# Moving the wait for the output's arrival from SyncE to the engine that owns the section

**Chip, cores, metric.** One core of a Trainium2 chip. The metric is the device time of one execution, in microseconds (us). Some words are used throughout. "Landing" is the moment when the last store's semaphore has its full count. A "section" is a stretch of the program in which each engine has its own list of instructions, and its "owner" is the engine that lets the others leave. An engine leaves with an "exit drain", an instruction that raises its "mark", a semaphore that the owner waits for. The "end barrier" is GpSimd's instruction, after the section, that waits for a count of all engines.

## The reference

Two decode steps of attention with one query token and 32 heads of 128. A reads all 16384 keys and values of its cache, B the last 4096 of its own. The two results, 512 numbers each, stand side by side.

```python
q = (x @ wq).reshape(B, Sq, Hq, Dh).transpose(0, 2, 1, 3)
scores = einsum("bhqd,bhkd->bhqk", q, k) * (Dh ** -0.5)
o = einsum("bhqk,bhkd->bhqd", softmax(scores), v)
y = o.transpose(0, 2, 1, 3).reshape(B, Sq, Hq * Dh) @ wo     # A: all keys; B: k, v cut to the last 4096
return concatenate([a, b], axis=-1)
```

## The kernel before

The kernel writes out each engine's instructions in one critical section with semaphores of its own, and names GpSimd as the section's owner. SyncE issues all large loads and, at the end, the two stores of 1 KB. GpSimd makes masks, then only passes semaphores on from VectorE to TensorE.

```python
ctx.enter_context(tc.tile_critical(sync_engine=mybir.EngineType.Pool))   # GpSimd (Pool) owns the section
...
def _sync_program(nc, cx, loads):
    e = nc.sync
    ...                                     # all loads of caches and weights
    for st in cx.sts:
        st.s_row.wait(e, len(st.out_at))
        cx.s_end.on(e.dma_start(out=cx.out[0, 0:1, st.at : st.at + st.DN],
                                in_=cx.row[0:1, st.at : st.at + st.DN]), 16)
    cx.s_end.wait(e, 32)                    # the wait that the change moves
...
def _pool_program(nc, cx):
    e = nc.gpsimd
    ...                                     # masks, zeros
    for i in range(stA.L + stB.L):
        m = _parts(i)
        for _ in range(m):
            n += 1
            cx.s_half.wait(e, n)            # wait and increment: one record of 17 ns
            e.sem_inc(cx.s_add.h, NB // m)
```

The softmax here doesn't subtract the row's maximum and nothing guards it: scores larger than these inputs give would overflow.

## Time and profile before

| | before |
|---|---|
| device time, median of 3 runs | 822.25 us (822.18 to 822.5) |
| span of the profiled run | 820.0 us |
| share of the 16 DMA engines' time filled by SyncE's queue | 99.4% |
| bytes moved | 352.41 MB at 430 GB/s |
| from the landing of the last store to the end of the span | 1.13 us |

What an engine does on leaving the section can be read in the view of one source line: engine, operation, count, then shortest, median and longest record in ns, and first and last start in us. The boundary's drains, no-ops and semaphore instructions are put down to L512.

```profile
L512 POOLq EVENT_SEMAPHORE  x3: 17/43/43, 778.3 to 819.1; - x3
L512 POOLq NOP  x2: 13/13/13, 0.8 to 819.2; - x2
L512 POOLq DRAIN  x1: 41/41/41, 778.4 to 778.4; - x1
L512 PEldq DRAIN  x1: 430/430/430, 816.9 to 816.9; - x1
L512 ACTq DRAIN  x1: 396/396/396, 817.3 to 817.3; - x1
L512 DVEq DRAIN  x1: 459/459/459, 817.3 to 817.3; - x1
L512 SPq DRAIN  x1: 13/13/13, 819.1 to 819.1; - x1
```

GpSimd (POOLq) runs its first boundary instruction and its own exit drain at 778.3 and 778.4 us, 40 us before the end. TensorE, ScalarE and VectorE drain at 817, while the output is still under way. Only SyncE's drain, at 819.1, stands behind the landing.

### The profile page before, as it was taken

The numbers are of one execution on the slowest core, as the hardware profiler recorded it, in microseconds if no ns is written. First come the engines' busy times: TensorE is split into PE (matmuls) and PEld (weight loads), VectorE is DVE, ScalarE is ACT, GpSimd is POOL, SyncE is SP. The second block draws the span as 40 slices with busy tenths as digits, with TensorE's granted clock in tenths as the row PEclk, the third lists the DMA queues.
The fourth block names the chain that finished last, engine by engine and source line by source line (L and its number), as shares of the span: only waits on it lengthen the run. The fifth ranks groups of instructions, "written<-read, shape, count | busy, mean of one in ns | idle before, by whom it ended". The sixth has DMA issues, their size and how long they took to land. (4 is left out here: it accounts for less than half of the span.)

```text
span 820.0 us, 5953 instructions
## 1 busy us (share of the span) xinstructions
PE 341.2 (42%) x2149; PEld 128.6 (16%) x2149; DVE 603.8 (74%) x167; ACT 35.5 (4%) x134; POOL 4.3 (1%) x14
## 2 busy tenths in 40 slices
PE   3433346152424244352608071534243353616276
PEld 1110112020101011110202020211011121202022
DVE  2089995959595968768595959595959969696921
ACT  0100000000000000000000000000000001010110
POOL 2000000000000000000000000000000000000000
PEclk9855668595856675656766575958566766756589
DMA  9999999999999999999999999999999999999997
GB/s 384 436 457 412 457 412 457 412 454 416 454 416 451 416 451 419 451 419 448 422 441 429 435 435 428 441 419 451 416 454 411 456 412 435 435 435 435 435 423 325
DMA packets 8222, 352.41 MB, mean 430 GB/s; under 512 B 916, under 2 KB 920, under 8 KB 1304
## 3 DMA queue, kind: packets, MB, share of 16 engines
q1 hardware_dynamic: 8212, 352.33, 99.4%
q8 instruction: 4, 0.07, 0.0%
q14 instruction: 2, 0.02, 0.0%
q10 hardware_dynamic: 4, 0.00, 0.0%
HBM read 352.32 MB, written 0.00 MB: 430 GB/s over the span
## 5 line engine op out<-in xcount | busy, mean ns | idle before, releaser
L304 DVE TENSOR_TENSOR kt<-kt,qallA 128x32768 bf16<-128x32768 bf16 (+2 forms) x20 | 276.2, 13810 | 150.7 <-DMA kt<-in_A_k_cache_dram 150.7
L379 PE MATMUL acc<-vt,p 128*8 128x512 bf16 (+1 forms) x1216 | 113.1, 550 | 348.3 <-PEq L42 348.3
L379 PE MATMUL red<-kt,ident 128*128 x640 | 183.2, 457 | 43.1 <-PEq L42 43.1
L315 DVE TENSOR_TENSOR kt<-kt 128x16384 bf16<-128x16384 bf16 (+2 forms) x24 | 174.5, 7269 | 0.8
L379 PEld LDWEIGHTS acc<-vt,p 128*8 128x8 bf16 (+1 forms) x1216 | 37.1, 114 | 423.5 <-issue 416.5
L379 PEld LDWEIGHTS red<-kt,ident 128*128 128x128 bf16 x640 | 72.5, 113 | 150.3 <-issue 103.6
L304 DVE TENSOR_TENSOR kt<-kt,qallB 128x16384 bf16<-128x16384 bf16 x8 | 69.5, 8691 | 13.4 <-DMA kt<-in_B_k_cache_dram 13.4
L321 DVE TENSOR_REDUCE sc<-red 128x256 f32<-128x2048 f32 x20 | 45.7, 2284 | 8.0 <-PE red L379 8.0
L233 ACT ACTIVATE p<-sc,offA 128x256 bf16<-128x256 f32 x32 | 16.0, 500 | 604.5 <-DVE sc L321 604.5
L379 PE MATMUL f<-s,win 128*32 128x128 f32 x48 | 11.2, 323 | 62.4 <-PEq L42 62.4
L379 PE MATMUL red<-vt,kt 128*128 128x512 bf16 x64 | 16.1, 416 | 4.6 <-DMA vt<-in_A_wq_dram 2.5
L233 ACT ACTIVATE p<-sc,offB 128x128 bf16<-128x128 f32 x32 | 12.4, 389 | 113.4 <-DVE sc L321 113.4
L342 DVE TENSOR_REDUCE s<-acc 128x128 f32<-128x512 f32 x24 | 16.6, 691 | 0.8
L379 PEld LDWEIGHTS f<-s,win 128*32 128x32 f32 x48 | 4.2, 121 | 72.9 <-issue 72.6
L337 DVE TENSOR_TENSOR acc<-acc,maskA 128x512 f32<-128x512 f32 x16 | 11.1, 692 | 0.0
L335 DVE COPY win<-selB 128x32 f32<-128x32 f32 x8 | 1.4, 178 | 11.3 <-PE acc L379 11.3
L379 PEld LDWEIGHTS red<-vt,kt 128*128 128x128 bf16 x64 | 6.6, 105 | 13.7 <-issue 7.8
L379 PE MATMUL red<-vt,ocA 128*1 128x512 bf16 x32 | 7.2, 379 | 0.0
L379 PE MATMUL acc<-kt,p 128*16 128x512 bf16 x64 | 5.3, 505 | 4.3 <-PEq L42 4.3
L335 DVE COPY win<-selA 128x32 f32<-128x32 f32 x16 | 2.8, 174 | 5.4 <-PE acc L379 5.4
L233 ACT ACTIVATION_READ_ACCUMULATOR p<-sc,offB 128x1 f32 x32 | 6.0, 187 | 0.0
L233 ACT ACTIVATION_READ_ACCUMULATOR p<-sc,offA 128x1 f32 x32 | 6.0, 187 | 0.0
(47 smaller groups left out, 36.8 us busy)
## 6 DMA issues: line engine op xcount, KB each, us to landing
kt<-in_B_k_cache_dram SPq DMA_DIRECT2D x8, 4096.0 KB, 34.8
vt<-in_B_v_cache_dram SPq DMA_DIRECT2D x6, 4096.0 KB, 29.0
kt<-in_B_v_cache_dram SPq DMA_DIRECT2D x2, 4096.0 KB, 36.6
vt<-in_A_wq_dram SPq DMA_DIRECT2D x1, 4096.0 KB, 12.2
vt<-in_B_wq_dram SPq DMA_DIRECT2D x1, 4096.0 KB, 21.4
vt<-in_A_wo_dram SPq DMA_DIRECT2D x2, 2048.0 KB, 23.1
vt<-in_B_wo_dram SPq DMA_DIRECT2D x1, 2048.0 KB, 29.7
vt<-in_B_wo_dram SPq DMA_DIRECT2D x1, 1024.0 KB, 31.6
```

The costliest lines, as they stand in the source:

```text
L233: ins = e.activation(out=p[:, :, g, :], in_=cx.sc[:, u * st.keys : (u + 1) * st.keys].rearrange("p (t e) -> p t e", e=4), func=ACT.Exp, sc ...
L304: n = did(e.tensor_tensor(out=k, in0=k, in1=q.rearrange("p (o d) -> p o d", o=1).broadcast_to([P, b - a, DH]), op=ALU.mult,))
L315: cx.s_half.on(e.tensor_tensor(out=k[:, :, 0 : DH // 2], in0=k[:, :, 0 : DH // 2], in1=k[:, :, DH // 2 : DH], op=ALU.add,))
L321: cx.s_sc.on(e.tensor_reduce(out=cx.sc[:, :], in_=cx.red[:, :, :].rearrange("p b (k w) -> p (b k) w", w=W), axis=AX.X, op=ALU.add,))
L335: did(e.tensor_copy(cx.win[u][:, :], st.sel[:, at : at + H]))
L337: n = did(e.tensor_tensor(out=acc, in0=acc, in1=st.mask[:, :].rearrange("p (x o) -> p x o", o=1).broadcast_to([P, 4, DH]), op=ALU.mult,))
L342: cx.s_pick.on(e.tensor_reduce(out=cx.s[u][:, :], in_=acc.rearrange("p x d -> p d x"), axis=AX.X, op=ALU.add,))
L379: mm = lambda *a, **k: e.matmul(*a, skip_group_check=True, **k)
```

## The change

Its intent: GpSimd closes the section, so let it wait for the output itself. SyncE then need not wait and tell GpSimd.

```diff
 def _sync_program(nc, cx, loads):
     ...
         cx.s_end.on(e.dma_start(...), 16)
-    cx.s_end.wait(e, 32)

 def _pool_program(nc, cx):
     ...
             e.sem_inc(cx.s_add.h, NB // m)
+    cx.s_end.wait(e, 32)
```

## The prediction

> **What bounds the kernel now.** I read the page first, for the engine that limits, then the chain of waits that ended last, then the waits of SyncE's queue, then stretches of the tail, and last the records of single instructions there.
>
> ```profile
> span 820.0 us, 5953 instructions
> PE 341.2 (42%) x2149; PEld 128.6 (16%) x2149; DVE 603.8 (74%) x167; ACT 35.5 (4%) x134; POOL 4.3 (1%) x14
> DMA  9999999999999999999999999999999999999997
> DMA packets 8222, 352.41 MB, mean 430 GB/s; under 512 B 916, under 2 KB 920, under 8 KB 1304
> ...
> q1 hardware_dynamic: 8212, 352.33, 99.4%
> ```
>
> All sixteen DMA engines are busy in every slice but the last, and SyncE's queue fills 99.4% of their time at 430 GB/s. The two caches and the weights are 352 MB: 352.41 MB / 430 GB/s = 819.6 us, which is the span. POOL (GpSimd) computes for 4.3 us of 820 and then only passes semaphores on. So the body is bound by bytes, and the change touches none of them. What it can move is the time after the last weight has landed:
>
> ```profile
> by line: DMA vt<-in_B_wo_dram 4.0%; PE acc L379 0.4%; SPq L171 0.3%; DVE row L373 0.1%; PE red L379 0.0%; issue 0.0%
> ...
> 784.12 32.74 DMA vt<-in_B_wo_dram
> 816.86 0.04 issue
> 816.90 0.40 PE red L379 x4
> 817.30 0.03 issue
> 817.33 0.42 DVE row L373
> ```
>
> The chain of what ended last stops at 817.75 us, where the last half row of B is in SBUF. Between that and 820.0 lie 2.25 us, in which the result is stored and the program closed.
>
> ```profile
> SPq L174 <- DVE row L373: 6.0, 1, 6.0
> SPq L132 <- DMA out_dram<-row: 0.9, 1, 0.9
> SPq L566 <- PEq L566: 0.5, 2, 0.4
> ...
> 817.00:818.00 1.00, 0.28 (x4) 0.00 (x0) 0.42 (x1) 0.37 (x1) 0.00 (x0) 1.00 0.00 0
> 818.00:819.00 1.00, 0.00 (x0) 0.00 (x0) 0.00 (x0) 0.00 (x0) 0.00 (x0) 1.00 0.00 1
> 819.00:820.00 1.00, 0.00 (x0) 0.00 (x0) 0.00 (x0) 0.00 (x0) 0.00 (x0) 0.74 0.00 0
> ```
>
> The first three lines are SyncE's queue: after its last issue (L174) it waits 0.9 us for the output's arrival, and this wait is attached to a branch printed as L132. In the last 2 us no compute engine does anything. The wait the change moves is 0.9 us out of 820, or 0.1%.
>
> [...] SyncE's branch has a record of only 33 ns although it had waited 0.9 us, so I count from start to start. [...] here the store took 818.874 - 817.772 = 1.10 us from issue to landing, so the measurement is used, and who waits cannot shorten it. [...] Here SyncE needs 160 ns from its branch to its next instruction, against 74 ns between its two later semaphore instructions, so a branch costs 86 ns more[...].
>
> **The change part by part.** The records of the semaphore instructions at the end, from the trace (start in us, length in ns; the meaning of each semaphore is my reading of who raises it and who waits):
>
> ```text
> GpSimd 778.248  17  last pass to TensorE
> GpSimd 778.326  17  raises "owner is through" (four engines' exit drains wait for it)
> GpSimd 778.422  41  its own exit drain, raises its mark
> SyncE  817.772 249  issues the store of B
>        818.874      both stores have landed
> SyncE  818.891  33  branch out of the section, held till then
> SyncE  819.051  13  exit drain, raises its mark (seen 819.065)
> GpSimd 819.089  43  second of two waits for the engines' marks (first: 817.831)
> GpSimd 819.176  13  no-op
> GpSimd 819.219  34  drain
> SyncE  819.353   7  drain, raises the end barrier's count (819.361)
> GpSimd 819.385  17  end barrier, has all the counts
>        820.004      last engine past the second end barrier
> ```
>
> The section's owner matters: GpSimd raises "owner is through" at the end of its own list, 40 us before the end, and the drains by which SyncE, ScalarE, VectorE and TensorE leave wait for it. Moving the wait into GpSimd's list puts it in front of that signal.
>
> Removed: SyncE's 0.9 us wait. Its branch and its 160 ns now follow the issue, from about 818.02 to 818.2, beside the store. SyncE's hop to GpSimd goes too: 819.089 - 819.051 = 38 ns.
>
> Added on GpSimd: a wait for 32 on the store's semaphore. I expect it to merge into the instruction that raises "owner is through", as each of the 24 earlier waits of that loop merged into one 17 ns record with its increment. It starts at 818.874 + 17 (SyncE's reaction) = 818.891.
>
> Moved behind the landing, GpSimd's line of instructions: the exit drain 96 ns later (778.326 to 778.422), 818.987. The first wait for marks about 85 ns later (the 34 ns drain at 819.743 is followed 78 ns later, this drain is 7 ns longer), 819.072. The second wait 87 ns later (as 819.089 to 819.176), 819.159. No-op 87, 819.246; drain 43, 819.289. The end barrier 78 ns after that, 819.367. Before it was 819.385. So the estimate is 18 ns earlier.
>
> Do the other engines' marks arrive in time? "Owner is through" goes out at 818.891; the end barrier's release, also raised by GpSimd, went from 819.464 to the waiters at 819.505 to 819.517, so 41 to 53 ns. The four drains start at 818.93 to 818.95, take about 10 ns as in the end barrier and are seen by 819.0: before GpSimd's waits at 819.07 and 819.16. Does SyncE then hold the barrier? From its drain at 818.93 to its count are 310 ns in the trace (819.051 to 819.361): 819.24, before 819.367. So GpSimd's line alone sets the end.
>
> Sum, both from 818.891. Old: 160 (branch) + 38 (hop) + 87 + 43 + 166 (from GpSimd's drain to the end barrier, 78 of it the usual gap and 88 spent waiting for SyncE's count) = 494 ns. New: 96 + 85 + 87 + 87 + 43 + 78 = 476 ns. Common to both are 87 + 43 + 78; what is saved is 160 + 38 + 88 = 286 ns, what is added is 96 + 85 + 87 = 268 ns. Change -0.02 us, with an error of some 0.1 us from the gaps I borrowed.
>
> **The rivals.**
> First, the handoff really is saved: if the exit marks and GpSimd's drain cost less than borrowed, or the author's idea holds that the owner has only its last no-op left, the gain is at most 819.176 - 818.891 = 0.285 us, 0.03%. The record of "owner is through" speaks against it.
> Second, the release costs more than it saves: the wait becomes an instruction of its own (+80 ns, the spacing of GpSimd's semaphore instructions), or an idle engine's exit drain is slow. TensorE took 430 ns, ScalarE 396, VectorE 459 in those drains, but each was then finishing real work; if they took that when idle, GpSimd would get its marks at 818.95 + 0.46 = 819.41 rather than 819.07, and the end moves by 0.25 us later, 822.5.
> Third, the change reaches the loads: if it shifted the instruction streams so that an issue came late, every percent of DMA idleness would be 8 us. The issues of the loads are the same instructions before the changed line, and the loads' waits are untouched; I give this almost nothing.
> Fourth, the end is hidden anyway: the measured 822.25 us is 2.25 us over the span[...].
>
> **Range and chances.** 822.25 - 0.02 rounds to 822.2 us. The rivals span 822.25 - 0.29 = 821.96 to about 822.5. The runs of before alone spread from 822.18 to 822.5, 0.32 us, so the state of a run is worth more than the effect. With 0.3 us added on each side the range is 821.7 to 822.8. A verdict of faster or slower needs 16 us, over fifty times what any rival makes: 0.005 each, 0.99 within 2%.
>
> **What would show it.** Right: the tail's records show GpSimd held until the store lands, the four exit drains starting together 40 to 50 ns later, SyncE's branch near 818.0 (on this trace's clock), its waits list without the 0.9 us on the output's arrival, and the end barrier within 0.1 us of 511 ns after landing (before: 819.385 - 818.874); DMA still at 99.4%. Wrong: exit drains that start before the landing (then the owner's signal isn't behind the wait), drains of hundreds of ns on idle engines, or a time outside 821.7 to 822.8 with the tail unchanged, which would put the cause in the loads or in the run itself.

Its sum: 494 ns for the old tail and 476 for the new, so -0.02 us and a forecast of 822.2 us.

## The result, and the profile after

| | before | after |
|---|---|---|
| device time, median of 6 runs | 822.26 us (822.0 to 822.5) | 822.3 us (822.2 to 822.48) |
| ratio | | 1.0001, 95% interval 0.9988 to 1.0014 |
| landing to end barrier, first profile | 511 ns | 688 ns |
| the same, second profile | 511 ns | 688 ns |

A ratio is the mean time of one kernel's fast runs over that of the other's of the same rounds, so not quite the ratio of the medians. The time is the same. The tail, the stretch from the landing to the end barrier, became 0.18 us longer, which is less than the spread of the runs.

First the page of the changed kernel:

```profile
span 820.5 us, 5953 instructions
PE 341.7 (42%) x2149; PEld 128.8 (16%) x2149; DVE 603.8 (74%) x167; ACT 35.5 (4%) x134; POOL 4.3 (1%) x14
DMA  9999999999999999999999999999999999999997
DMA packets 8222, 352.41 MB, mean 430 GB/s; under 512 B 916, under 2 KB 920, under 8 KB 1304
...
q1 hardware_dynamic: 8212, 352.33, 99.3%
```

As many instructions, as many packets, the same busy times to a few tenths of a microsecond: the body didn't change. The span is 0.45 us longer in this profile, but its last result (the end of "row") already came 0.27 us later, at 818.02 against 817.75, ahead of anything that was changed. A second profile of the kernel before has a span of 820.7 us. Spans of the body wander by such amounts, and the tail has to be measured from the landing.

The waits of SyncE's queue after the change:

```profile
SPq L174 <- DVE row L373: 5.4, 1, 5.4
SPq L512 <- POOLq L512: 1.1, 1, 1.1
...
SPq L566 <- PEq L566: 0.7, 2, 0.4
```

The 0.9 us on the output's DMA are gone, and in their place SyncE waits 1.1 us for GpSimd at the section's boundary. The wait was not removed but turned: SyncE now waits for the engine that waits for the store. The store itself took 1.10 us from issue to landing in the first profile of either kernel. The branch that carries the wait, and the boundary's line, both of the changed kernel:

```profile
L132 POOLq COMPARE_BRANCH  x1: 33/33/33, 819.2 to 819.2; - x1
```

```profile
L512 POOLq EVENT_SEMAPHORE  x3: 17/43/43, 819.3 to 819.6; - x3
L512 POOLq NOP  x2: 13/13/13, 0.8 to 819.7; - x2
L512 SPq DRAIN  x1: 13/13/13, 819.4 to 819.4; - x1
L512 ACTq DRAIN  x1: 8/8/8, 819.4 to 819.4; - x1
L512 DVEq DRAIN  x1: 17/17/17, 819.4 to 819.4; - x1
L512 PEldq DRAIN  x1: 8/8/8, 819.4 to 819.4; - x1
L512 POOLq DRAIN  x1: 41/41/41, 819.4 to 819.4; - x1
```

Compare the starts with those of before. Everything that stood at 778 or 817 us now stands at 819.3 or later: GpSimd's first signal, its drain, and the drains of all four other engines, which that signal releases (they start 42 to 53 ns after it). The drains of TensorE, ScalarE and VectorE have become short, 8 to 17 ns instead of 396 to 459. In the kernel before, those of ScalarE and VectorE ended 35 and 52 ns after the engine's last operation; now the last operation is over 1.3 us before them. They cost little: the other engines' marks are all raised by 252 ns after the landing, and GpSimd's first wait for them starts only at 389. GpSimd's own row of instructions is what costs, 516 ns from its signal to the end barrier.

The single records, counted in ns from the landing, show the sum:

```text
before: SyncE waits                       after: GpSimd waits
   17  SyncE   branch                       24  GpSimd  branch
  177  SyncE   exit drain                  172  GpSimd  raises "owner is through"
  215  GpSimd  second wait for marks       214  SyncE   exit drain (others: 218 to 225)
  302  GpSimd  no-op                       268  GpSimd  exit drain
  345  GpSimd  drain                       389  GpSimd  first wait for marks
  511  GpSimd  end barrier                 480  GpSimd  second wait for marks
                                           567  GpSimd  no-op
                                           610  GpSimd  drain
                                           688  GpSimd  end barrier
```

### The profile page after: what moved, and what is told of

It reads as the page before. It is cut to its first block, busy times and chain, and to the rows that moved or that the text cites. A ratio compares the mean times of both kernels' runs of the same rounds, so it can differ in the third digit from the quotient of the medians.

```text
span 820.5 us, 5953 instructions
## 1 busy us (share of the span) xinstructions
PE 341.7 (42%) x2149; PEld 128.8 (16%) x2149; DVE 603.8 (74%) x167; ACT 35.5 (4%) x134; POOL 4.3 (1%) x14
## 2 busy tenths in 40 slices
DMA packets 8222, 352.41 MB, mean 430 GB/s; under 512 B 916, under 2 KB 920, under 8 KB 1304
## 3 DMA queue, kind: packets, MB, share of 16 engines
q1 hardware_dynamic: 8212, 352.33, 99.3%
## 5 line engine op out<-in xcount | busy, mean ns | idle before, releaser
L379 PE MATMUL acc<-vt,p 128*8 128x512 bf16 (+1 forms) x1216 | 111.3, 543 | 350.0 <-PEq L42 350.0
L379 PE MATMUL red<-vt,kt 128*128 128x512 bf16 x64 | 18.2, 455 | 4.6 <-DMA vt<-in_A_wq_dram 2.5
```

The lines of the kernel that those rows point to most:

```text
L379: mm = lambda *a, **k: e.matmul(*a, skip_group_check=True, **k)
```

## The experiments

The theory: behind the landing stands a row of sequencer instructions with fixed distances, and the owner that waits puts its whole row there. Rivals: the two tails differ by chance; GpSimd alone is slow; the tail is hidden by the closing of the program. For edits of a single line the diff is against the kernel named.

### before_again and after_again: is the tail's length chance?

No edit, one look each.

> The kernel before once more, for the repeatability of its tail. Theory 1 (the tail is fixed instruction spacing): from the landing of the last store to GpSimd's end barrier 511 ns as in the first profile, within 20 ns, whatever the span does. Theory 2 (the tail is as noisy as the span, and the 511 against 688 ns of the two first profiles is chance): it differs from 511 by 50 ns or more.

> The changed kernel once more. Theory 1: 688 ns from landing to end barrier, within 20 ns. Theory 2: it differs from 688 by 50 ns or more, perhaps down to 511.

Measured: 511 and 688 ns, as in the first profiles, to the nanosecond, while the times were 822.8 and 822.4 us, the wrong way round. So single runs can't rank these kernels, and the tail can.

### owner_plain and sync_plain: what does the branch cost?

```diff
# owner_plain, against the changed kernel; sync_plain: the same in SyncE's list, against the kernel before
     cx.s_end.wait(e, 32)
+    e.sem_inc(cx.s_own.h, 1)    # nobody waits for it
```

> GpSimd waits, but an increment of a semaphore that nobody waits on follows the wait, so that the wait sits on a plain semaphore instruction and not on the branch out of the section. Theory 1 (the branch is what the prediction mis-sized, 148 ns from its start to the next instruction against 78 for a plain one): landing to end barrier 688 - 70 = 618 ns, no branch record on GpSimd. Rival (GpSimd is slow to leave a wait of any kind): stays within 20 ns of 688, or gets longer by the added instruction's 78 ns.

> The kernel before with the same added increment after SyncE's wait. Theory 1: SyncE's 160 ns from its branch to its exit drain become about 75 to 95 ns, landing to end barrier 511 - 75 = 436 ns, within 25 ns: the shortest tail so far. Rival: 511 or more, since the added instruction costs what the branch did.

Measured: 618 and 416 ns, with times of 822.25 and 822.51 us. In owner_plain the wait sits on a 17 ns semaphore record and the next instruction follows after 78 ns instead of 148; the rest keeps its distances. In sync_plain SyncE's drain follows after 74 ns instead of 160. So in these kernels an instruction added makes the tail shorter: the wait that was last in its list sat on the branch out of the section, and the branch cost 70 ns more than the increment on GpSimd (148 - 78) and 86 on SyncE (160 - 74). But the owner's tail without the branch (618) is still above the old one with it (511), so the branch is only part of the 177 ns: with the branch gone on both sides, 618 against 416, the owner's tail is still 202 ns longer.

### owner_tail26 and owner_ahead26: does the tail reach the measured time?

```diff
# owner_tail26, against the changed kernel; in owner_ahead26 the loop stands ahead of the wait
     cx.s_end.wait(e, 32)
+    for _ in range(26):
+        e.sem_inc(cx.s_own.h, 1)
```

> GpSimd waits, then does 26 increments that nobody waits on. Theory 1 (GpSimd's instructions behind the landing reach the measured time one for one): landing to end barrier 688 - 148 + 26 x 78 = 2.57 us, the time 1.9 us over the changed kernel, 824.2 us. Rival (the end of the program is hidden behind the launch's own closing): the time stays within 0.5 us of 822.3.

> The same 26 increments ahead of GpSimd's wait, where it is idle for 40 us. Both theories: landing to end barrier 688 ns within 20, time 822.3 within 0.4 us. If it were longer, the number of instructions and not their place would count.

Measured over 4 runs each: owner_tail26 824.23 us (824.14 to 824.32), ratio to before 1.0024, interval 1.0008 to 1.0039; owner_ahead26 822.22 us (821.87 to 822.51), ratio 1.0001. The tails are 2949 and 693 ns. The same 26 instructions cost 2.0 us behind the landing and nothing ahead of it, so the tail isn't hidden. One line of SyncE's waits in owner_tail26 says it:

```profile
SPq L514 <- POOLq L514: 3.3, 1, 3.3
```

SyncE waits 3.3 us for the owner's signal, where it waited 1.1 in the changed kernel. The tail of 2949 ns missed the expected 2570: the increments follow one another by 78 ns, but after the same one of them, the twenty-first, the next comes 441 ns later in both kernels. The traces show where it stands. Counted from the start of the trace, this is the step after GpSimd's 68th record, behind the landing in one kernel and 39 us ahead of it in the other. The two kernels with twelve sections, below, have a long step after the 68th record as well (440 ns where GpSimd waits, 424 where SyncE waits), and the first of them has another, of 403 ns, after the 196th, 128 records on. The other kernels have at most 61 records of GpSimd and no such step. So in these four kernels the place went by the count of GpSimd's records, 68, and not by where the landing lay; that such a step comes again after 128 records was seen once. What fills the gap was not shown: both kernels with 26 increments moved one packet more on queue 14, which the page marks "instruction", than the kernel before (3 instead of 2, 8192 bytes each), but it began 0.69 us after the gap's end in owner_tail26 and 4.25 us after it in owner_ahead26. The time grew by 2.0 us where the tail grew by 2.26; the difference of 0.25 us is within the spread of the four runs.

### twelve_sync and twelve_owner: thirteen exits instead of one

```diff
# after the main section, in both; the last line's engine is nc.sync or nc.gpsimd,
# and the main section is that of the kernel before or of the changed one
+    section.close()
+    for r in range(1, 13):
+        with tc.tile_critical(sync_engine=mybir.EngineType.Pool):
+            for e in (nc.vector, nc.scalar, nc.tensor, nc.gpsimd):
+                e.sem_inc(cx.s_own.h, 1)
+            cx.s_end.on(nc.sync.dma_start(out=..., in_=cx.row[...]), 16)     # B's half again
+            cx.s_end.wait(nc.sync, 32 + 16 * r)
```

> Twelve more sections at the end, each storing B's half of the output again, with an increment on every other engine so that all five take part; SyncE waits for each store, as before. The result stays right. Theory 1: each section costs issue and landing (1.1 us), exit and entry, about 2 us, so some 24 us more than before, near 846 us. The number wanted is the difference from the next run.

> The same twelve sections, with GpSimd waiting for each store. Theory 1 (0.18 us per exit, the whole of it on the path and in the time): 13 x 0.177 = 2.3 us longer than twelve_sync. Rival A (what the exit loses, the next entry gives back, or it lies beside something outside the span): within 0.5 us of twelve_sync. Rival B (the author's intent, a saved hop): shorter than twelve_sync.

Measured over 5 runs each: 842.94 us (842.82 to 843.38; ratio to before 1.0253, interval 1.0239 to 1.0267) and 846.64 us (846.53 to 847.25; ratio 1.0296, interval 1.0282 to 1.031). The owner's wait is slower by 3.70 us. The direction is that of the theory and the effect now stands clear of the spread; Rivals A and B fall. The size was expected at 2.3 us. In the traces the distance from a landing to the next section's store is 622 ns with SyncE waiting and 892 with GpSimd (median of 12), so 270 ns for exit and entry rather than 177 for exit and end barrier: 12 x 0.27 = 3.2 us. The last exit adds 0.6 us (1069 against 466 ns from landing to end barrier), for in twelve_owner the gap of 403 ns lies ahead of its no-op, where the exits before it have 87 to 92. Together that is 3.8 us in the profiled runs, of which 0.3 are this gap; it stands after GpSimd's 196th record, and that it has to do with the wait is not shown. Also here the waits of SyncE's queue, first twelve_sync, then twelve_owner:

```profile
SPq L544 <- DMA out_dram<-row: 10.4, 12, 1.0
```

```profile
SPq L544 <- POOLq L544: 12.8, 12, 1.1
...
SPq L574 <- POOLq L544: 3.7, 12, 0.3
```

Twelve waits for the store, 10.4 us together, became twelve for GpSimd, 12.8 us, and twelve further ones of 0.3 us for GpSimd's mark at the next entry, which the list of twelve_sync doesn't have.

### sync_owner and act_waits: the role or the engine?

```diff
# sync_owner, against the kernel before
-    ctx.enter_context(tc.tile_critical(sync_engine=mybir.EngineType.Pool))
+    ctx.enter_context(tc.tile_critical(sync_engine=mybir.EngineType.SP))
# act_waits, against the kernel before: the wait taken out of SyncE's list, to the end of ScalarE's
+    cx.s_end.wait(e, 32)
```

> SyncE owns the section and waits itself: owner and waiter are one engine, as in the changed kernel, but the engine is SyncE. Theory 1 (what counts is that the owner's release of the four exit drains, and its own exit line, stand behind the wait): the same order of records as in the changed kernel, drains of the other engines after the landing, landing to end barrier about 570 ns (17 + 150 + 90 + 3 x 74 + 60 + 8 + 24), more than the 511 of before and less than 688, since SyncE's instructions follow one another faster. Rival (GpSimd alone is the trouble, an owner that waits is no worse): 511 or less.

> GpSimd owns the section, ScalarE waits for the stores in SyncE's place. Theory 1 (a waiter that doesn't own the section leaves the owner's release and exit drain early): landing to end barrier 511 within 60 ns, GpSimd's owner signal near 778 us as in before. Rival (SyncE alone can wait cheaply): nearer to 688.

Measured: 655 and 388 ns, times of 822.31 and 822.41 us. In sync_owner the records have the order of the changed kernel: SyncE's branch at 17 ns, its signal at 180, the others' drains at 218 to 225, its own row up to 630, the end barrier at 655. GpSimd's drain, at 778 us in the kernel before, stands behind the landing (819.0) here too:

```profile
L512 SPq EVENT_SEMAPHORE  x3: 17/28/28, 819.2 to 819.4; - x3
L512 POOLq DRAIN  x1: 41/41/41, 819.2 to 819.2; - x1
```

That another engine as waiting owner is also slower than 511 says that the role matters, not GpSimd's speed alone. The expected 570 ns, which counted on SyncE's steps of 74 ns where GpSimd's took 78 (both in the kernel before), was too low. act_waits fell outside its expected 511 within 60 ns, on the short side. There SyncE's own closing row, which GpSimd's end barrier waited for until 479 ns in the kernel before, runs beside the store nearly to its end: only two drains are left, and its last count goes out at 316 ns. So the changed kernel's idea, to free SyncE of the wait, does shorten the tail, but in these runs it took a waiter that isn't the owner.

### act_plain: the two helpful edits together

```diff
# against act_waits
     cx.s_end.wait(e, 32)
+    e.sem_inc(cx.s_own.h, 1)
```

> The two helpful edits together: ScalarE waits (it owns nothing, and SyncE's own closing list then lies beside the store), and an increment follows the wait, so that it doesn't sit on the branch. Theory 1: 388 ns from landing to end barrier less the branch's 156 - 78 = 78 ns, so 310 ns within 25: the shortest tail of all, 0.2 us below the kernel before and 0.38 below the changed one. In the measured time 0.2 us are less than the spread of the runs (0.4 us), so the verdict is same, 822.1 us within 0.4. Rival: GpSimd or SyncE becomes the last, 360 ns or more.

Measured: 320 ns, the shortest tail of all. ScalarE's branch had taken 156 ns to the next instruction, the increment in its place took 88: the 68 ns between 388 and 320. In time 822.17 us (821.91 to 822.26, 5 runs), ratio to before 0.9998, interval 0.9984 to 1.0012: the same. No version beats the kernel before by anything that its time shows. Its boundary line:

```profile
L513 POOLq EVENT_SEMAPHORE  x3: 17/43/712, 778.5 to 818.5; - x3
L513 POOLq NOP  x2: 13/13/13, 0.8 to 819.3; - x2
L513 POOLq DRAIN  x1: 41/41/41, 778.6 to 778.6; - x1
...
L513 SPq DRAIN  x1: 218/218/218, 818.3 to 818.3; - x1
L513 ACTq DRAIN  x1: 8/8/8, 819.2 to 819.2; - x1
```

GpSimd's signal and drain are back at 778 us, SyncE's drain is at 818.3, before the landing at 819.1, and of the exit drains only ScalarE's, of 8 ns, stands behind it. The record of 712 ns is GpSimd's second wait for marks, SyncE's and ScalarE's; in act_waits this record, there of 778 ns, runs from 24 ns after SyncE's mark to 30 ns after ScalarE's. So this wait for two semaphores lies inside its record, while SyncE's branch in the kernel before waited 0.9 us and has a record of 33 ns. A record's start, from which the prediction counts, is here not the moment of the last mark.

The tails side by side:

| run | waits | owns | wait sits on | landing to end barrier |
|---|---|---|---|---|
| after, after_again | GpSimd | GpSimd | branch | 688 ns |
| sync_owner | SyncE | SyncE | branch | 655 ns |
| owner_plain | GpSimd | GpSimd | increment | 618 ns |
| before, before_again | SyncE | GpSimd | branch | 511 ns |
| sync_plain | SyncE | GpSimd | increment | 416 ns |
| act_waits | ScalarE | GpSimd | branch | 388 ns |
| act_plain | ScalarE | GpSimd | increment | 320 ns |

## Why the prediction was right, and which step of it was not

- **The bound**: right. The body is bound by bytes: DMA share 99.3 against 99.4%, the same packets, the same time within 0.04 us of medians. 822.3 us lies in the range of 821.7 to 822.8, and 822.2 was the forecast. That these two agree says nothing of the tail: runs of one kernel spread by 0.3 us and more, and a tail of +0.18 us in place of -0.02 can't be seen in them. As far as the tail goes, the number was luck.
- **The tail's change of -0.02 us**: wrong in sign; it is +0.18 us. The sign of being right that the prediction had set, an end barrier within 0.1 us of 511 ns after the landing, was missed at 688. From the landing the prediction had 17 + 96 + 85 + 87 + 87 + 43 + 78 = 493 ns (17 of reaction and its 476), and 688 were measured. The step that failed is "I expect it to merge into the instruction that raises 'owner is through'": the wait sat on a branch of its own, and the signal followed 148 ns later. By owner_plain, 78 of these are for an instruction of its own and 70 for its being the branch. The trace of before held a warning: SyncE's wait, also the last of its list, sits there on a branch (818.891) and did not merge into the exit drain behind it. The rest are mis-sized gaps: from the exit drain to the first wait 121 ns, not "about 85" (why is not shown), the reaction 24 and not 17, and 91 not 87 between the two waits. 148 + 36 + 7 + 4 = 195 = 688 - 493.
- **The release behind the wait**: right. The drains started 42 to 53 ns after the signal (40 to 50 predicted), lasted 8 to 17 ns, and SyncE's count came 301 ns after its drain (310) and did not set the end. So GpSimd's row alone does, as predicted.
- **Rivals**: the first, a saving of up to 0.285 us, fell. The second was right in direction: the wait got an instruction of its own, dearer than its 80 ns; its other half, slow drains on idle engines, fell (8 to 17 ns; its sum was also short: marks at 819.41 rather than 819.07 would have moved GpSimd's row by 0.34 us, not 0.25). The third, a reach to the loads, is not seen: 8222 packets in both, queue share 99.3%. The fourth, a tail that doesn't show, fell with owner_tail26.
- **SyncE's branch near 818.0**: not seen. With no wait on it, it left no record in the changed kernel (L132 lists GpSimd's alone), as GpSimd's left none before the change.

## What to carry to other kernels

Let an engine that does not own the section wait for the last store, and one whose own closing row is short: ScalarE in SyncE's place cut the tail from 511 to 388 ns. (In the changed kernel ScalarE's row from its exit drain on went from 218 to 305 ns after the landing, SyncE's from 214 to 513.) The owner's signal released the others, 42 to 53 ns later in the changed kernel and 38 to 45 in sync_owner, so a wait put ahead of it put their exits and the owner's own behind the landing. In a kernel of 822 us bound by bytes none of this shows; with one short section after another it was 0.27 us for each.
